# Fewer and larger DMA issues on the SyncE queue in the attention stage of an attention and expert kernel

## The chip, the cores and the metric

The kernel runs on one core of one Trainium2 chip. The metric is the device time of one execution in microseconds (us); the median of several executions is compared.

## The reference, cut to what matters

Eight heads of causal attention over 8 batches of 576 rows, four heads with a local mask (the last 32 positions) and four with a strided one (positions of the same residue modulo 32); the result is the input of a layer of 8 experts, of which each row takes one.

```
scores = scale * q @ k.T                                   # 8 batches, 8 heads, 576 x 576, head size 64
mask_local   = (rel >= 0) & (rel < 32)                      # heads 0 to 3
mask_strided = (rel >= 0) & (pos_k % 32 == pos_q % 32)      # heads 4 to 7
attn = softmax(where(mask, scores, -1e9)); x = (attn @ v) as 4608 rows of 512
e = argmax(x @ w_gate)                                      # one expert a row
out = gate * sigmoid(x @ w_output_gate)[e] * relu(x @ w1[e]) @ w2[e]
```

## The kernel before, in words

The attention stage is a hand-ordered pipeline (the schedule is manual: every engine executes its instructions in the order in which the program writes them). It has 40 steps, t = 0 to 39: batch b = t // 5, and within a batch j = t % 5. A step deals with two windows (w = 0, 1) of up to 128 packed rows. Steps j = 0 and 1 hold strided rows only, j = 3 and 4 local rows only; in j = 2 the first window is strided, and the second holds 64 local and 36 strided rows.

At step t the loop in `attention` (lines 637 to 681) writes, among others: the scores of step t on TensorE (`scores`, L267, into the PSUM tile sp); the normalization of step t-4 on VectorE (`norm`, L329 to L334), which gives the tile x_t; the storing of x_t into the DRAM tensor xd (`rows`, L346 for local rows, L350 for strided rows, on the SyncE queue, called SP); the mask and the maximum of step t on VectorE (`bar` L279, `top` L286); the subtraction on GpSimd (L293), the exponential on ScalarE (L298), the product with the values for step t-3 (`values`, L319), and transposes for later steps. In steps j = 3 and 4 the local values of the batch, one half of the heads each, are copied from vlt to vev, shifted by half a tile (`even`, L229), by VectorE and by ScalarE. Chains for the gate of the experts (`logits`, `gating`) are woven in by `pump`.

The inputs of a batch are read by SP too (`load`, L203): ks and kl (strided and local keys, two halves), qs and ql (strided and local queries, two halves, both into the tile q_t), vs and vl (strided and local values, two halves). All but vl are read for the batch that follows, and there are two buffers of each. `PLAN` says which load is issued in which step and in which part of it: part 2 is at the head of the step (`begin(t, 2)`, L642), parts 0 and 1 stand in `rows` behind the stores of window 0 and window 1. In the steps before t = 4, which have no rows to store, `begin` is called directly. In steps 1 to 4 SP also writes initial entries into the table of rows by expert (`clear`, L97, eight times).

Behind attention come the expert layers: `layer1` (L790), `layer2` (L806) and the scatter of their rows (L823). They read xd by gathers.

Of the kernel before, what the change touches and what calls it, by code (L numbers as in the profile page):

```python
# [17 lines left out]
B, H, S, D = 8, 8, 576, 64  # L18
# [13 lines left out]
NS = 5  # L32
# [20 lines left out]
def attn_moe_kernel(  # L53
# [19 lines left out]
    nc = tc.nc  # L73
# [21 lines left out]
    def clear(e):  # L95

        nc.sync.dma_start(out=table.rearrange("(e p a) w -> e p (a w)", e=E, p=128)[e], in_=empty[0])  # L97
# [68 lines left out]
    def attention():  # L166
        with ExitStack() as actx:
# [20 lines left out]
            def load(b, what, n=None, cs=None):  # L188

                hd = slice(0, 2) if n is None else slice(n, n + 1)  # L190
                cs = cs or slice(0, WS if what == "qs" else S)
                i = b % 2
                if b not in qts:
                    qts[b] = inp.tile([128, 4, WS], F32, name="q_t")
                dst, src = {
                    "ks": lambda: (kbs[i][n::2, :, n, cs], ks[b, n, :, :, cs]),
                    "qs": lambda: (qts[b][:, 2 + hd.start:2 + hd.stop, cs], qs[b, :, hd, cs]),
                    "kl": lambda: (kbl[i][n::2, :, n, :], kl[b, n]),
                    "ql": lambda: (qts[b][:, hd, 0:S], ql[b, :, hd]),
                    "vs": lambda: (vst[i][n::2, n], vs[b, n]),  # L200
                    "vl": lambda: (vlt[i][n::2, n], vl[b, n]),
                }[what]()
                nc.sync.dma_start(out=dst, in_=src)  # L203

            PLAN = {(0, 0): [(1, "ks", 0)], (0, 1): [(1, "ks", 1)], (0, 2): [(0, "vl", 0)],
# [4 lines left out]

            def begin(t, s):
                for d, what, n in PLAN.get((t % NS, s), []):
                    if 0 < t // NS + d < B:
                        load(t // NS + d, what, n)

            zeros = xe[:, 0, 0:256]

# [7 lines left out]
            def even(b, eng, h, f):  # L225

                ps = slice(64 * f, 64 * (f + 1))
                copy = nc.scalar.copy if eng is nc.scalar else eng.tensor_copy
                copy(out=vev[ps, h, f:NL].rearrange("p n i e -> p (n i e)"),  # L229
                     in_=vlt[b % 2][ps, h, 0:NL - f].rearrange("p n i e -> p (n i e)"))  # L230
# [3 lines left out]
            def tiles(j, w):  # L234

                u = 2 * j + w
                local = [(32 * a, 4 * (u - 6) + 2 + a) for a in range(4)] if u > 5 else [(0, 0), (32, 1)] if u == 5 else []
                strided = [(64 * h, 2 * u + 1 + h) for h in range(2)] if u < 5 else [(64, 0)] if u == 5 else []
                return [(p0, 32, n) for p0, n in local] + [(p0, 64, g) for p0, g in strided]
# [98 lines left out]
            def rows(b, j, t=None):  # L338
                x_t = x_[b, j]
                dst = xd[b * S:(b + 1) * S, :]  # L340
                for w in range(2):
                    ts = tiles(j, w)
                    nl = sum(m for _, m, _ in ts if m == 32)
                    if nl:
                        q0 = 32 * ts[0][2]
                        nc.sync.dma_start(out=dst[q0:q0 + nl, 0:256], in_=x_t[0:nl, w, :])  # L346
                    for p0, m, g in ts:
                        if m == 64:
                            r0, nr = resid(g)
                            nc.sync.dma_start(  # L350
                                out=dst[:, 256:512].rearrange("(i r) f -> i r f", r=STRIDE)[:, r0:r0 + nr],
                                in_=x_t[p0:p0 + R * nr, w, :])
                    if t is not None:
                        begin(t, w)

            def resid(g):
                return (0, 2) if g == 0 else (3 * g - 1, 3)
# [225 lines left out]
            def pump():  # L583
                clock[0] += 1
                k = clock[0]
                for c in chains:
                    if k >= c[1]:
                        try:
                            n, z = next(c[0]), 1
                            while n == 0 and (now[0] >= B * NS or z < Z):  # L590
                                n, z = next(c[0]), z + 1
                            c[1] = k + 1 + max(n, 0)
                        except StopIteration:
                            c[1] = 1 << 30
                chains[:] = [c for c in chains if c[1] < 1 << 30]
# [40 lines left out]
            t = 0  # L636
            while t < ns:
                now[0] = t
                live = lambda k: 0 <= t - k < ns
                at = lambda fn, k, *a: fn((t - k) // NS, (t - k) % NS, *a) if live(k) else None  # L640
                b, j = t // NS, t % NS
                begin(t, 2)  # L642
                if 0 < t < 5:
                    clear(2 * t - 2)
                    clear(2 * t - 1)
                at(scores, 0)
                at(norm, 4, 0)
                at(evac_x, 5)
                pump()
                at(norm, 4, 1)  # L650
                pump()
                at(norm, 4, 2)
                if live(4):
                    at(rows, 4, t)
                else:
                    begin(t, 0)
                    begin(t, 1)
                at(bar, 0)
                at(values, 3)
                at(top, 0)  # L660
                at(shift, 0)
                at(turn_p, 2)
                at(turn_x, 4)
                at(evac_p, 2)
                pump()
                pump()
                for h in ((0,) if b and j == 3 else (1,) if b and j == 4 else (0, 1) if t == 4 else ()):
                    even(b, nc.scalar, h, 1)
                    even(b, nc.vector, h, 0)
                at(expo, 0)  # L670
                if t in WIPES:
                    wipe(*WIPES[t])
                if t + 1 < len(WARM):
                    warm(WARM[t + 1])
                pump()
                pump()
                if live(XL) and (t - XL) % NS > 2:
                    chains.append([logits((t - XL) // NS, (t - XL) % NS - 3), 0])
                pump()
                pump()  # L680
                t += 1
# [358 lines left out]
```

## Time and profile before

| | |
|---|---|
| median of 3 runs | 673.96 us (668.85 to 674.24) |
| profiled execution | 675.84 us |
| its span from first to last instruction | 674.1 us |
| mean granted TensorE clock | 0.988 |
| busy share of the span | TensorE 95%, VectorE 46%, ScalarE 40%, GpSimd 29% |

The profile is of one execution. "Busy" leaves out waiting, and DMA issues aren't counted as busy. The 40 slices of the page are 16.85 us each. PE stands for TensorE's matmuls, PEld for its weight loads, DVE for VectorE, ACT for ScalarE, POOL for GpSimd and SPq for SyncE's queue, whose instructions here are issues of DMAs. L12 is line 12 of the kernel.

### The profile page before, as it was taken

The numbers are of one execution on the slowest core, as the hardware profiler recorded it, in microseconds if no ns is written. First come the engines' busy times: TensorE is split into PE (matmuls) and PEld (weight loads), VectorE is DVE, ScalarE is ACT, GpSimd is POOL, SyncE is SP. The second block draws the span as 40 slices with busy tenths as digits, with TensorE's granted clock in tenths as the row PEclk, the third lists the DMA queues.
The fourth block names the chain that finished last, engine by engine and source line by source line (L and its number), as shares of the span: only waits on it lengthen the run. The fifth ranks groups of instructions, "written<-read, shape, count | busy, mean of one in ns | idle before, by whom it ended". The sixth has DMA issues, their size and how long they took to land.

```text
span 674.1 us, 13235 instructions
## 1 busy us (share of the span) xinstructions
PE 639.0 (95%) x5109; PEld 542.4 (80%) x5109; DVE 310.3 (46%) x676; ACT 270.6 (40%) x491; POOL 192.9 (29%) x196
## 2 busy tenths in 40 slices
PE   7889998898898999999999999999999999999995
PEld 5667776777676888988798879889988987987984
DVE  6568887887574224423243224234434423531510
ACT  5755556555543224333333323234234323432410
POOL 5224556556544402201320130024024013111011
PEclk9899999999997999999999999999999999999998
DMA  9977888789342735514251433245245324431001
GB/s 271 347 221 212 259 249 238 243 247 315 95 131 78 226 103 150 162 32 141 85 155 44 132 110 124 77 124 166 64 122 171 98 87 119 144 108 41 2 13 41
DMA packets 47849, 96.86 MB, mean 144 GB/s; under 512 B 9076, under 2 KB 19844, under 8 KB 47786
## 3 DMA queue, kind: packets, MB, share of 16 engines
q1 hardware_dynamic: 38330, 72.58, 36.2%
q0 software_dynamic: 8048, 20.05, 8.9%
q10 hardware_dynamic: 1408, 3.38, 1.5%
q8 instruction: 41, 0.67, 0.4%
q14 instruction: 22, 0.18, 0.1%
HBM read 74.44 MB, written 22.38 MB: 144 GB/s over the span
## 4 chain that ended last, share of the span: by engine, by line
PE 56%; issue 21%; DVE 6%; DMA 6%; POOL 5%; ACT 3%; SPq 1%; POOLq 0%; DVEq 0%; ACTq 0%
PE yp L806 23%; PE hp L790 21%; PE xp L319 4%; DMA q_t<-in_qs_dram 3%; PE sp L267 2%; POOL out_dram L823 2%; PE tp L780 2%; PE tp L305 1%; DVE p_t L279 1%; DVE st L286 1%; POOL xg L151 1%; PE xtp L364 1%; DMA vlt<-in_vl_dram 1%; PE gp L396 1%; POOL p_t L293 1%
## 5 line engine op out<-in xcount | busy, mean ns | idle before, releaser
L790 PE MATMUL hp<-xh,w1l 128*128 128x256 f32 (+1 forms) x480 | 147.9, 308 | 0.0
L790 PE MATMUL hp<-xl,w1h 128*128 128x256 f32 (+1 forms) x480 | 147.8, 308 | 0.0
L790 PE MATMUL hp<-xh,w1h 128*128 128x256 f32 (+1 forms) x480 | 147.8, 308 | 0.0
L823 POOL DMA_INDIRECT out_dram<-ys,tab x40 | 41.9, 1046 | 353.4 <-ACT ys L822 342.1
L790 PEld LDWEIGHTS hp<-xh,w1h 128*128 128x128 f32 x480 | 91.0, 190 | 2.1
L790 PEld LDWEIGHTS hp<-xl,w1h 128*128 128x128 f32 x480 | 91.0, 190 | 1.9
L790 PEld LDWEIGHTS hp<-xh,w1l 128*128 128x128 f32 x480 | 90.9, 189 | 1.4
L806 PE MATMUL yp<-w2h,hhb 128*128 128x512 f32 (+3 forms) x208 | 83.9, 403 | 0.0
L806 PE MATMUL yp<-w2l,hhb 128*128 128x512 f32 (+3 forms) x208 | 82.0, 394 | 0.0
L806 PE MATMUL yp<-w2h,hlb 128*128 128x512 f32 (+3 forms) x208 | 81.6, 393 | 0.0
L728 DVE TENSOR_TENSOR xl<-tp,xh 128x512 fp32r<-128x512 f32 (+3 forms) x40 | 25.7, 650 | 120.0 <-ACT xh L727 119.8
L727 ACT CAST xh<-tp 128x512 fp32r<-128x512 f32 (+3 forms) x40 | 21.9, 555 | 130.4 <-PE tp L780 130.4
L794 DVE SCALAR_TENSOR_TENSOR hlb<-hp,hhb 128x480 fp32r<-128x480 f32 (+7 forms) x64 | 34.6, 541 | 84.6 <-ACT hhb L793 84.6
L793 ACT ACTIVATE hhb<-hp 128x480 fp32r<-128x480 f32 (+7 forms) x64 | 30.6, 478 | 102.8 <-PE hp L790 102.8
L293 POOL TENSOR_TENSOR p_t<-p_t,st 128x512 f32<-128x512 f32 x40 | 47.4, 1186 | 75.2 <-DVE st L286 20.1
L806 PE MATMUL yp<-w2h,hha 128*128 128x512 f32 x128 | 52.1, 407 | 0.0
L806 PE MATMUL yp<-w2h,hla 128*128 128x512 f32 x128 | 51.3, 400 | 0.0
L151 POOL DMA_INDIRECT xg<-xd,tab x40 | 46.7, 1168 | 15.6 <-issue 10.1
L806 PE MATMUL yp<-w2l,hha 128*128 128x512 f32 x128 | 51.1, 399 | 0.0
L563 POOL DMA_INDIRECT table<-meta,dst x48 | 44.7, 931 | 20.8 <-issue 10.2
L794 DVE SCALAR_TENSOR_TENSOR hla<-hp,hha 128x256 fp32r<-128x256 f32 x56 | 23.6, 421 | 54.8 <-ACT hha L793 54.8
L822 ACT ACTIVATE ys<-yp,tab 128x512 f32<-128x512 f32 (+3 forms) x40 | 27.7, 693 | 48.2 <-issue 28.5
(147 smaller groups left out, 1076.9 us busy)
## 6 DMA issues: line engine op xcount, KB each, us to landing
raw<-in_moe_w_dram SPq DMA_DIRECT2D x54, 512.0 KB
vst<-in_vs_dram SPq DMA_DIRECT2D x16, 357.5 KB
vlt<-in_vl_dram SPq DMA_DIRECT2D x16, 292.5 KB
xd<-x_t SPq DMA_DIRECT2D x80, 54.0 KB
q_t<-in_qs_dram SPq DMA_DIRECT2D x14, 293.0 KB
xd<-x_t SPq DMA_DIRECT2D x32, 128.0 KB
q_t<-in_ql_dram SPq DMA_DIRECT2D x14, 288.0 KB
raw<-in_moe_w_dram ACTq DMA_DIRECT2D x6, 512.0 KB
```

What stands on the lines that cost most here:

```text
L151: nc.gpsimd.indirect_dma_start(out=dst, out_offset=None, in_=src, in_offset=bass.IndirectOffsetOnAxis(ap=idx, axis=0), bounds_check=top, o ...
L293: nc.gpsimd.tensor_tensor(out=p_t, in0=p_t, in1=st.unsqueeze(2).to_broadcast([128, 4, 64, 2]), op=ALU.subtract)
L319: nc.tensor.matmul(out=xp[p0:p0 + m, w, 130 * i:130 * (i + 1)], lhsT=pt[:, w, i, p0:p0 + m], rhs=value(b, i, m, n), start=True, stop=True)
L563: i = nc.gpsimd.indirect_dma_start(out=table[:, :], out_offset=bass.IndirectOffsetOnAxis(ap=dst[:, j:j + 1], axis=0), in_=meta[:, b * NB + ...
L727: nc.scalar.copy(out=hi, in_=src)
L728: nc.vector.tensor_tensor(out=lo, in0=src, in1=f32(hi), op=ALU.subtract)
L790: nc.tensor.matmul(out=hp[:, 0:n], lhsT=w[:, k, 128 * j:128 * (j + 1)], rhs=x[:, k, 0:n], start=first, stop=(k == KC - 1 and w is w1l))
L793: nc.scalar.activation(out=hh[:, j, 0:n], in_=hp[:, 0:n], func=AF.Relu)
L794: nc.vector.scalar_tensor_tensor(out=hl[:, j, 0:n], in0=hp[:, 0:n], scalar=0.0, in1=f32(hh[:, j, 0:n]), op0=ALU.max, op1=ALU.subtract)
L806: nc.tensor.matmul(out=yp[0:m, :], lhsT=h[:, j, o:o + m], rhs=w[:, j, :], start=(j == 0 and q == 0), stop=(j == FC - 1 and q == 2))
L822: nc.scalar.activation(out=ys[0:m, :], in_=yp[0:m, :], func=AF.Copy, scale=f32(tab[:, 1:2]))
L823: i = nc.gpsimd.indirect_dma_start(out=out[:, :], out_offset=bass.IndirectOffsetOnAxis(ap=tab[:, 0:1], axis=0), in_=ys[0:m, :], in_offset= ...
```

## The change: larger loads and stores, and a new order

Three things are done. The local rows of the steps j = 3 and j = 4, two windows of 128 rows, are stored by one DMA instead of two. The two halves of the strided queries of a batch are one load, and so are the two halves of the local queries. The loads of a batch, now ten, are dealt out anew, one to each of the two parts 0 and 1 of the five steps; part 2, at the head of a step, is gone. The local rows of a step are now stored ahead of its strided rows.

```
-            PLAN = {(0, 0): [(1, "ks", 0)], (0, 1): [(1, "ks", 1)], (0, 2): [(0, "vl", 0)],
-                    (1, 0): [(1, "qs", 0)], (1, 1): [(1, "qs", 1)], (1, 2): [(0, "vl", 1)],
-                    (2, 0): [(1, "kl", 0)], (2, 1): [(1, "kl", 1)],
-                    (3, 0): [(1, "ql", 0)], (3, 1): [(1, "ql", 1)],
-                    (4, 0): [(1, "vs", 0)], (4, 1): [(1, "vs", 1)]}
+            PLAN = {(0, 0): (1, "ks", 0), (0, 1): (0, "vl", 0), (1, 0): (1, "ks", 1), (1, 1): (0, "vl", 1),
+                    (2, 0): (1, "qs", None), (2, 1): (1, "kl", 0), (3, 0): (1, "kl", 1), (3, 1): (1, "ql", None),
+                    (4, 0): (1, "vs", 0), (4, 1): (1, "vs", 1)}
 
             def begin(t, s):
-                for d, what, n in PLAN.get((t % NS, s), []):
-                    if 0 < t // NS + d < B:
-                        load(t // NS + d, what, n)
+                d, what, n = PLAN[t % NS, s]
+                if 0 < t // NS + d < B:
+                    load(t // NS + d, what, n)
...
             def rows(b, j, t=None):
                 x_t = x_[b, j]
                 dst = xd[b * S:(b + 1) * S, :]
+                if j > 2:
+                    q0 = 256 * j - 704
+                    nc.sync.dma_start(out=dst[q0:q0 + 256, 0:256].rearrange("(w p) f -> p w f", w=2), in_=x_t)
+                elif j == 2:
+                    nc.sync.dma_start(out=dst[0:64, 0:256], in_=x_t[0:64, 1, :])
                 for w in range(2):
-                    ts = tiles(j, w)
-                    nl = sum(m for _, m, _ in ts if m == 32)
-                    if nl:
-                        q0 = 32 * ts[0][2]
-                        nc.sync.dma_start(out=dst[q0:q0 + nl, 0:256], in_=x_t[0:nl, w, :])
-                    for p0, m, g in ts:
+                    for p0, m, g in tiles(j, w):
                         if m == 64:
                             r0, nr = resid(g)
                             nc.sync.dma_start(
...
                 b, j = t // NS, t % NS
-                begin(t, 2)
                 if 0 < t < 5:
                     clear(2 * t - 2)
```

## Rows read from the trace of the kernel before

**Rows 1.** The page: busy time, share of the span and instructions of each engine; then the granted TensorE clock and the busy share of the DMA engines in 40 equal slices, in tenths.

```profile
PE 639.0 (95%) x5109; PEld 542.4 (80%) x5109; DVE 310.3 (46%) x676; ACT 270.6 (40%) x491; POOL 192.9 (29%) x196
...
PEclk9899999999997999999999999999999999999998
DMA  9977888789342735514251433245245324431001
```

**Rows 2.** The chain of work that ended last, in order of time: start, duration (us), what. A DMA's piece goes from its issue to its landing.

```profile
18.79 4.95 DMA q_t<-in_qs_dram
...
41.31 4.57 DMA q_t<-in_qs_dram
...
103.05 5.35 DMA q_t<-in_qs_dram
...
218.72 20.93 PE hp L790 x96
```

**Rows 3.** The timeline of TensorE, the scores of the steps 5, 10 and 20 to 25: start, duration (us), engine, line, operation, tiles, shapes, count; in brackets the idle time before it and what ended it.

```profile
23.13 0.44 PE L267 MATMUL sp<-kbs,q_t 128*64 128x128 f32 x4 [2.58 <-DMA q_t<-in_qs_dram]
23.77 1.55 PE L267 MATMUL sp<-kbs,q_t 128*64 128x128 f32 x12 [0.20 <-DMA q_t<-in_qs_dram]
...
43.09 0.44 PE L267 MATMUL sp<-hha,q_t 128*64 128x128 f32 x4
45.92 0.88 PE L267 MATMUL sp<-hha,q_t 128*64 128x128 f32 x12 [2.39 <-DMA q_t<-in_qs_dram]
...
86.59 1.09 PE L267 MATMUL sp<-hha,q_t 128*64 128x128 f32 x16
...
90.58 1.10 PE L267 MATMUL sp<-hha,q_t 128*64 128x128 f32 x16
...
94.75 1.09 PE L267 MATMUL sp<-hha,q_t 128*64 128x128 f32 x12
...
98.82 1.08 PE L267 MATMUL sp<-hla,q_t 128*32 128x128 f32 x32
...
103.09 1.06 PE L267 MATMUL sp<-hla,q_t 128*32 128x128 f32 x32
...
107.09 0.44 PE L267 MATMUL sp<-kbs,q_t 128*64 128x128 f32 x4
108.44 0.88 PE L267 MATMUL sp<-kbs,q_t 128*64 128x128 f32 x12 [0.91 <-DMA q_t<-in_qs_dram]
```

**Rows 4.** SP's issues by line, over the whole span: the line, the transfer and the number of issues; the time that an issue took (least, median, most, in ns); the start of the first and the last (us). L203 is loads, L350 strided rows, L346 local rows.

```profile
L203 SPq DMA_DIRECT2D q_t<-in_qs_dram x16: 397/458/1663, 0.9 to 144.3; - x16
L203 SPq DMA_DIRECT2D vst<-in_vs_dram x16: 532/534/808, 6.9 to 156.5; - x16
L203 SPq DMA_DIRECT2D vlt<-in_vl_dram x16: 524/538/1392, 8.2 to 163.1; - x16
L203 SPq DMA_DIRECT2D q_t<-in_ql_dram x15: 424/464/1097, 4.9 to 151.2; - x15
...
L203 SPq DMA_DIRECT2D kbs<-in_ks_dram x8: 552/589/593, 13.5 to 139.5; - x8
...
L350 SPq DMA_DIRECT2D xd<-x_t x88: 725/758/1645, 26.1 to 180.6; - x88
...
L346 SPq DMA_DIRECT2D xd<-x_t x40: 319/492/2452, 39.9 to 183.8; - x40
```

**Rows 5.** The timeline of SP: start, duration (us) of an issue, line, transfer, count. The first is the load of all local queries of batch 0 in one issue.

```profile
4.90 0.61 SPq L203 DMA_DIRECT2D q_t<-in_ql_dram  x1
...
26.07 1.72 SPq L350 DMA_DIRECT2D xd<-x_t  x2
...
82.79 0.46 SPq L203 DMA_DIRECT2D q_t<-in_qs_dram  x1
...
98.13 1.33 SPq L203 DMA_DIRECT2D vlt<-in_vl_dram  x1
99.56 1.59 SPq L350 DMA_DIRECT2D xd<-x_t  x2
...
104.67 2.45 SPq L346 DMA_DIRECT2D xd<-x_t  x1
```

**Rows 6.** Windows of the attention stage: the stretch, its length, the busy time of each engine (instructions), the granted clock, the share of the DMA engines and what they moved (GB/s).

```profile
24.00:28.00 4.00, 4.00 (x36) 3.46 (x35) 1.62 (x4) 1.29 (x3) 0.97 (x1) 0.61 1.04 403
...
87.00:108.00 21.00, 18.90 (x303) 14.78 (x298) 17.65 (x49) 12.46 (x28) 12.15 (x13) 1.00 0.84 248
```

**Rows 7.** DMA issues by size: the table's clears and the stores of local rows.

```profile
xd<-x_t SPq DMA_DIRECT2D x32, 128.0 KB
...
table<-raw SPq DMA_DIRECT2D x8, 296.0 KB
```

**Rows 8.** The timeline of VectorE: the copies of the local values in the steps 8 and 9, the x_t of step 21, and the second copy of the local values of batch 4, in step 24.

```profile
38.05 0.75 DVE L229 COPY vev<-vlt 64x1170 f32<-64x1170 f32 x1
...
41.62 0.75 DVE L229 COPY vev<-vlt 64x1170 f32<-64x1170 f32 x1
...
91.86 0.69 DVE L334 TENSOR_TENSOR x_t<-xp,rs 128x512 f32<-128x512 f32 x1
...
105.63 0.75 DVE L229 COPY vev<-vlt 64x1170 f32<-64x1170 f32 x1
```

## Prediction

> **What bounds the kernel now.** I read the page first. TensorE is busy for 95% of the span, and its granted clock is full in nearly every slice [rows 1]. The DMA digits are 7 to 9 in the first ten slices and, but for one, 0 to 5 behind them [rows 1], so there are two stages: attention, up to about 190 us, and the expert layers behind it. The chain in order of time confirms the second: from 218.72 us on it runs through matmuls of the experts [rows 2]. Nothing of the change is left there, so I count it unchanged.
>
> In attention the chain is carried by matmuls and VectorE, but at a few places it passes through a strided query load that had not landed: issued at 18.79, at 41.31 and at 103.05 us, landing 4.95, 4.57 and 5.35 us later [rows 2]. The timeline of TensorE shows the price of each: the scores of steps 5, 10 and 25, each the first step of a batch, stood for 2.58 + 0.20, 2.39 and 0.91 us [rows 3]. These 6.1 us are all that late loads cost TensorE.
>
> Between them the loop keeps a beat of its own: 86.59, 90.58, 94.75, 98.82, 103.09, 107.09 us are the starts of six successive scores [rows 3], that is 3.99 + 4.17 + 4.07 + 4.27 + 4.00 = 20.50 us a batch without a stall. In such a batch TensorE works 18.9 and VectorE 17.65 of 21 us [rows 6]; no load is in that beat.
>
> Why do those loads come late? SP's timeline: the second query half is issued at 82.79 and again at 103.05 us [rows 2, 5], 20.26 us for 28 issues. By the medians [rows 4] these are 2 x (0.458 + 0.534 + 0.538 + 0.464) + 4 x 0.589 (keys) = 6.34 us of loads, 11 strided stores x 0.758 = 8.34, 5 local stores x 0.492 = 2.46: 17.14 us. The other 3.1 us, 0.11 an issue, are gaps and issues that took long without a cause that I can read, as the 2.45 us and the 1.33 us [rows 5]. So SP issues for 20.26 of 20.50 us and never catches up: the x_t written at 91.86 + 0.69 = 92.55 us [rows 8] gets its first store issued at 99.56 [rows 5], 7.0 us later. The queue is late, not the engines short of transfers: their share is 0.84 there [rows 6].
>
> **The change part by part.** *Fewer issues.* Per batch 28 become 24: two local stores, one query half of each kind. In the whole kernel 8 x 2 + 7 x 2 = 30. What the merged ones cost is not in the trace; the whole local query load of the start is one issue of 0.61 us [rows 5] against 2 x 0.464, and I take 0.61 for both merged queries. The merged store has a third dimension: at least a local store (0.492), at most two of them (0.98); I take 0.70, near the strided one at 0.758, which also has an extra dimension. Then SP has 5.72 + 8.34 + 0.49 + 2 x 0.70 = 15.95 us and 24 x 0.11 = 2.64: 18.6 us a batch. It gains 20.5 - 18.6 = 1.9 us a batch on the loop; if the merged ones cost as much as their two halves, only 0.45 + 0.24 = 0.7. By itself this is worth nothing: SP is waited for through late loads alone.
>
> *Start, step 5.* The strided queries of batch 1 move from step 1 to step 2, behind two more table clears of 296 KB [rows 7]. The DMA engines are full there (share 1.04, 403 GB/s [rows 6]), so two clears are 2 x 303 / 403 = 1.5 us. The second half landed at 23.7 us; the whole one lands at 25.2. Also, all 16 matmuls of the scores now wait for it; before, four ran at 23.13, the rest from 23.77 to 25.32 [rows 3]. All 16 take 1.09 us [rows 3], so they end at 25.3 + 1.1 = 26.4: **+1.0 us** at step 5, with bounds 0 and +2.9 (the clears' bandwidth halved by what else is queued).
>
> The wait for both halves is where a page speaks against the change. The trace shows matmuls of the first query half running at 23.13 and 43.09 us while the second had not landed [rows 3]. The Trainium skill, "DMA: Bandwidth & Descriptors", section "Why a DMA increments its semaphore by 16 and not by 1", says that only the full count tells that a transfer has landed, so nothing of a merged load can be used early. By that rule the four matmuls lose their head start, 0.4 us at a step that waits; the sum above has it.
>
> *Step 10.* SP's 20 issues from 26.07 us [rows 5] up to this load are 20 in both kernels. In the new order they are 11 strided stores (8.34), two loads each of vs, vl and ks (3.32), one local and one merged store (1.19), with gaps of 0.06 to 0.11 14.1 to 15.1 us; in the start two issues fewer stand ahead, up to 0.5 us earlier. The whole query load is issued at 39.7 to 41.2. It lands after 4.57 to 5.35 us, as the halves did [rows 2], plus the second half's 300 KB at 403 down to 248 GB/s [rows 6], 0.7 to 1.2 us: between 45.0 and 47.8. I take 45.8, near the middle, since the low ends belong to a queue without long issues. Before, the second half released 12 matmuls at 45.92 which took 0.88; now 16 follow 45.8 with 1.09: **+0.1 us**, bounds -0.7 and +2.1. The +1.0 of step 5 disappears in this wait: the loop would ask at 43.09 + 1.0 = 44.1, before the landing.
>
> *Local values, steps 8 and 9.* Their loads move from the head of a step to its end, behind four stores and a key load: 4 x 0.758 + 0.589 = 3.6 us, and gaps. They are issued at about 34.2 and 38.4 us and land (4.57 to 5.35) at 38.8 to 39.6 and 43.0 to 43.7. The copies to vev asked at 38.05 and 41.62 [rows 8], now 1.0 later: 39.05 and 42.6. So the second may hold up VectorE, and ScalarE's copy behind it, by 0.4 to 1.1 us; queued behind them are the normalization, the mask of step 10 and the exponential. Step 10's scores wait for queries until 45.8 anyway: **0**, and up to 1.1 if that cover is gone.
>
> *Step 25.* Three batches later SP has gained 3 x 1.9 = 5.7 us (bounds 2.1 and more), the whole load needs up to 1.2 more. The 0.91 us of stall go in full: **-0.9 us**. With the lower bounds it is 2.1 - 1.2 = 0.9, just enough. What is late next is nothing: the beat of 20.50 us goes on.
>
> *Moved loads with no effect.* Second half of the strided keys a step later, local keys a half step, local queries at the end of step 3: each has two steps (8 us) or more to its use, against some 5 us of landing. Local rows ahead of strided rows: both wait for the same x_t, and its buffer is asked for five steps later, 20.5 us.
>
> Sum: +0.1 - 0.9 = -0.8 us on a span of 674.1 (the profiled execution took 675.84, so 675.0). That execution was 1.9 us above the median; I put the sum on the median: 673.96 - 0.8 = **673.1 us**.
>
> **The rivals.** *SP stays late, values come late (slower).* If SP gains nothing, for instance because long issues scale with the size of a transfer, the local values are the trap. The second half was issued at 98.13 and used at 105.63 [rows 5, 8]: 7.5 us, of which landing takes 4.57 to 5.35, so 2.2 to 2.9 are left. Issued 3.6 us later it is 0.7 to 1.4 us late, in each of the batches 1 to 7, in front of VectorE's and ScalarE's queues: 7 x 1.05 = 7.4, with step 25's stall kept: about 681 us. It decides where SP gains less than about 1 us in all by then. Against it: 30 issues less, and a beat that needs 20.50 where SP would need 18.6.
>
> *All waits go (faster).* If a merged load lands as fast as a half and the start's clears don't delay it, the 2.58 + 0.20 + 2.39 + 0.91 go: 668 us, no more, since the beat stays. Against it: the DMA engines are full when step 5's load is queued [rows 6]. The Trainium skill's page just named, section "Rules for kernel authors", advises to coalesce small transfers since overhead dominates them; by it this case would be the likely one. The trace does not bear it out: issues follow each other every 0.5 to 0.8 us while each takes 4.6 us or more to land [rows 2, 4], so their fixed parts overlap.
>
> *No effect.* The stall of step 10 only shifts, that of step 25 stays: 674 us.
>
> **How the numbers follow.** Chances: forecast 0.72, no effect 0.13, all waits go 0.08, SP stays late 0.07. A change of this kernel under about 1% can't be told from none (the runs shown lie 0.8% apart); forecast, no effect and nearly all of the faster case are inside it, and half of the slower case: within 1% 0.92, faster 0.03, slower 0.05. The range: the forecast's bounds are -0.7 - 0.9 = -1.6 and +2.1 + 1.1 = +3.2; the low runs of before, 5 us under the median, and the faster case pull the lower end to 669.0; the upper end is 677.2.
>
> **What would show it.** Right: scores of step 5 start some 2 us later than 23.13, step 10's end near 47 as before, no stall on a query load after it; the lag between x_t and its first store shrinks from 7 us to about the wait for x_t itself by 110 us; 24 issues per batch, 18 to 19 us of SP. Wrong: waits of VectorE or ScalarE on the local values beyond step 9, a beat other than 20.5 us, a merged store that takes over 1 us to issue, or a second stretch at the lower of the two clock levels after the longer stop of TensorE at step 5 (24 to 28 us has a granted clock of 0.61 now [rows 6]; as much again would cost 4 x 0.39 = 1.6 us).

## The result and the profile after

The changed kernel takes 676.14 us (median of 20 executions, 673.06 to 680.05), the kernel before 673.34 us beside it (20 executions): ratio 1.0059, 95% interval 1.0041 to 1.0076. It is 2.8 us slower where 0.8 us of gain were forecast; the time lies inside the range, the sign is wrong.

The profiled execution took 675.56 us with a span of 673.9 us, no more than the one of before (675.84 and 674.1). The two traces can't be subtracted from end to end: the profiled execution of before lay 2.5 us above its median, and each execution has its own stretches of lower clock, as shown below. So I compare stage by stage. One execution of the runs below (of ids_before), at 1044.44 us with a granted clock of 0.557, is a slow one and left out of its ratio. The page of the changed kernel, TensorE's busy time, then the granted clock in 40 slices [rows 1]:

```profile
PE 637.9 (95%) x5109; PEld 541.6 (80%) x5109; DVE 310.9 (46%) x676; ACT 270.5 (40%) x491; POOL 192.4 (29%) x196
...
PEclk9799999999998999999999999999999999999998
```

The timeline of TensorE in the changed kernel, the scores (L265) of the steps 5, 10, 11, 25 and 35 to 37 and one matmul in between; in brackets the idle time before and what ended it [rows 3]:

```profile
25.50 1.98 PE L265 MATMUL sp<-kbs,q_t 128*64 128x128 f32 x16 [5.08 <-DMA q_t<-in_qs_dram]
...
45.47 1.09 PE L265 MATMUL sp<-hha,q_t 128*64 128x128 f32 x16
...
49.46 1.10 PE L265 MATMUL sp<-hha,q_t 128*64 128x128 f32 x16
...
107.03 1.09 PE L265 MATMUL sp<-kbs,q_t 128*64 128x128 f32 x16
...
148.64 1.09 PE L265 MATMUL sp<-kbs,q_t 128*64 128x128 f32 x16
...
153.64 1.09 PE L265 MATMUL sp<-kbs,q_t 128*64 128x128 f32 x16
...
157.25 0.27 PE L317 MATMUL xp<-vev,pt 128*32 128x130 f32 x1 [2.52 <-DVE x_t L332]
...
159.31 0.88 PE L265 MATMUL sp<-kbs,q_t 128*64 128x128 f32 x10
```

The same places in the kernel before, from step 35 on:

```profile
149.69 1.09 PE L267 MATMUL sp<-kbs,q_t 128*64 128x128 f32 x16
153.68 1.10 PE L267 MATMUL sp<-kbs,q_t 128*64 128x128 f32 x16
156.17 0.27 PE L319 MATMUL xp<-vev,pt 128*32 128x130 f32 x1 [1.40 <-DVE x_t L334]
158.23 1.09 PE L267 MATMUL sp<-kbs,q_t 128*64 128x128 f32 x12
```

At step 35 the changed kernel is 149.69 - 148.64 = 1.05 us ahead, near the 0.8 us forecast. Two steps later it is 1.08 us behind: 8.54 us became 10.67. No load ends a wait there. The place to look at is GpSimd, whose subtraction every step needs. GpSimd in the kernel before, then in the changed one, from step 32 on: the read of the small table `tabe` for the step ahead (DMA_DIRECT2D), the subtractions of steps 33, 34 and 36 (TENSOR_TENSOR), and scatters into `table`:

```profile
142.38 0.59 POOL L453 DMA_DIRECT2D tabe<-table  x1 [0.56 <-issue]
144.51 1.46 POOL L293 TENSOR_TENSOR p_t<-p_t,st 128x512 f32<-128x512 f32 x1 [1.53 <-DVE dst L556]
146.49 0.95 POOL L563 DMA_INDIRECT table<-meta,dst  x1 [0.52 <-DVE x_t L334]
147.75 1.33 POOL L563 DMA_INDIRECT table<-meta,dst  x1 [0.31 <-issue]
149.10 1.05 POOL L293 TENSOR_TENSOR p_t<-p_t,st 128x512 f32<-128x512 f32 x1
...
158.58 1.06 POOL L293 TENSOR_TENSOR p_t<-p_t,st 128x512 f32<-128x512 f32 x1
```

```profile
141.92 0.59 POOL L451 DMA_DIRECT2D tabe<-table  x1 [1.14 <-issue]
143.46 1.46 POOL L291 TENSOR_TENSOR p_t<-p_t,st 128x512 f32<-128x512 f32 x1 [0.95 <-DVE dst L554]
147.98 0.95 POOL L561 DMA_INDIRECT table<-meta,dst  x1 [3.06 <-DVE st L284]
149.24 0.92 POOL L561 DMA_INDIRECT table<-meta,dst  x1 [0.30 <-DMA q_t<-in_ql_dram]
150.19 1.05 POOL L291 TENSOR_TENSOR p_t<-p_t,st 128x512 f32<-128x512 f32 x1
...
159.66 1.06 POOL L291 TENSOR_TENSOR p_t<-p_t,st 128x512 f32<-128x512 f32 x1
```

The read is issued 0.46 us earlier than before, yet GpSimd stands 3.06 us ahead of the scatter that follows, where it was 0.52. The releasers printed there are others. The scatter writes the table that the read reads, and waits for it; the profile has no row of the landing, so I read it from the trace's semaphore events. The last of the read's 16 increments comes at 145.66 us before and 147.15 after, 3.28 and 5.23 us behind the issue, and GpSimd's wait on that semaphore, a separate instruction ahead of the scatter, ends 0.03 us later in both; it lasted 1.15 us before and 3.68 after. From that scatter on GpSimd has no slack: subtraction 34 to subtraction 36 takes 9.48 and 9.47 us, filled with four scatters and two gathers, so whatever the read loses arrives at step 37.

The second place is the start. Windows of 22 to 32 us, before and after (columns as in [rows 6]; the clock stands behind the five engines):

```profile
22.00:32.00 10.00, 8.59 (x101) 6.89 (x101) 5.23 (x12) 6.84 (x11) 1.62 (x2) 0.83 1.01 371
```

```profile
22.00:32.00 10.00, 6.50 (x60) 5.56 (x60) 3.07 (x6) 4.37 (x8) 1.04 (x1) 0.66 0.98 348
```

TensorE stood for 5.08 us ahead of step 5, and the lower of the two clock levels (1.2 of 2.4 GHz) was granted from 22.94 to 29.77 us instead of 23.71 to 27.12: 6.83 us against 3.41.

### The profile page after: what moved, and what is told of

It reads as the page before. It is cut to its first block, busy times and chain, and to the rows that moved or that the text cites. A ratio compares the mean times of both kernels' runs of the same rounds, so it can differ in the third digit from the quotient of the medians.

```text
span 673.9 us, 13205 instructions
## 1 busy us (share of the span) xinstructions
PE 637.9 (95%) x5109; PEld 541.6 (80%) x5109; DVE 310.9 (46%) x676; ACT 270.5 (40%) x491; POOL 192.4 (29%) x196
## 4 chain that ended last, share of the span: by engine, by line
PE 45%; issue 20%; POOL 3%; DMA 1%; POOLq 0%
PE yp L803 23%; PE hp L787 21%; POOL out_dram L820 2%; PE tp L777 2%; POOL xg L151 1%; DMA xg<-xd,tab 1%; POOL table L561 0%; POOLq L820 0%; POOLq L905 0%; POOLq L151 0%
```

## The experiments

All ratios are to the kernel before on the same chip. In the list, t5, t11 and t35 are the starts of the scores of these steps, "35-37" the time from scores 35 to scores 37, "read" the landing of tabe's read behind its issue, "low" the time at the lower clock ahead of the experts' first full layer (us, one trace each). The three runs on a chip where the kernel before took 701.71 us don't stand in it:

```
kernel          ratio  [95%]             t5     t11    t35     35-37  read  low
before          1                        23.13  49.54  149.69   8.54  3.28  10.2
before_again                             22.70  50.30  149.47   8.54  3.48   6.8
before_third                             23.87  50.00  149.14   8.46  3.18   6.8
rows_only       1.0004 [0.9988, 1.0020]  23.71  49.04  148.23   8.53  3.39   3.4
queries_only    0.9997 [0.9972, 1.0021]  23.62  47.23  146.41  11.26  4.53   6.8
old_order       0.9998 [0.9977, 1.0018]  23.47  48.49  147.66  10.72  4.85   6.8
after           1.0059 [1.0041, 1.0076]  25.50  49.46  148.64  10.67  5.23  10.2
after_again     1.0058 [1.0036, 1.0079]  24.86  48.93  148.06  10.48  4.66  10.2
early_queries   1.0062 [1.0036, 1.0088]  23.00  50.93  150.07  11.88  4.67  10.2
late_weights    1.0044 [1.0021, 1.0068]  25.35  49.52  148.68  11.28  4.44  13.7
halves          1.0071 [1.0046, 1.0097]  25.14  50.44  149.56  10.57  5.13   6.8
swap_last       1.0050 [1.0030, 1.0070]  25.41  49.91  149.03  12.00  5.00  13.7
swap            1.0053 [1.0031, 1.0075]  24.11  48.72  147.82  11.08  4.35  13.7
tabe_early      1.0025 [1.0011, 1.0040]  25.49  52.91  152.07  10.40  2.85   6.8
ids_after       1.0007 [0.9990, 1.0023]  26.24  51.02  150.14   8.27    -    3.4
ids_before      0.9986 [0.9968, 1.0004]  22.64  47.78  146.92   8.26    -    3.4
free_old_again  0.9973 [0.9953, 0.9994]  22.49  46.25  145.41   8.25  4.71   0.0
```

**The change again, and its parts at the start.** The changed kernel as it is:

> The changed kernel once more, for a second trace and a measured ratio beside the experiments. Theory A (the start pays): step 5 starts again near 25.5 us instead of 23.1, behind two more table clears, with a stretch at the lower clock level of some 6.8 us instead of 3.4; ratio to the kernel before about 1.004 to 1.006. Theory B (the end of attention pays): the GpSimd read of the table (tabe) lands 5 us after its issue instead of 3.3, the subtraction of step 34 starts more than 5 us after its scores instead of 3.4, and steps 36 and 37 come 2 us later relative to step 34. In the one trace of the changed kernel both are seen; a second one tells whether they are there each time.

The table clears of steps 1 to 4 behind the step's loads:

```
-                if 0 < t < 5:
-                    clear(2 * t - 2)
-                    clear(2 * t - 1)
...
                     begin(t, 1)
+                if 0 < t < 5:
+                    clear(2 * t - 2)
+                    clear(2 * t - 1)
```

> The changed kernel, but in steps 1 to 4 SP writes the table clears behind the loads of the step instead of ahead of them, so the whole strided query load of batch 1 has two clears ahead of it, as its second half had before. Theory A: step 5 starts at 23.5 to 24.0 us instead of 25.5, the stretch at the lower clock is 3.4 us, and the time falls by 2 to 3 us against the changed kernel (ratio to before 1.000 to 1.002). Theory B: step 5 is earlier by as much, but the time falls by less than 1 us unless the lead survives the GpSimd waits at steps 34 to 37.

The four loads of the first weights, in the step ahead, each issued a step later:

```
-                for c in range(4):
-                    if c > 1:
+                for c in range(5):
+                    if c in (2, 3):
...
-                    load_w(0, 1, cs=[c])
+                    if c:
+                        load_w(0, 1, cs=[c - 1])
```

> The changed kernel, but the four loads of the first expert's weights (L160, 512 KB each), which start beside the GpSimd read of the table, are issued one step later. Theory B: the read of the table lands 3 to 4 us after its issue, the subtraction of step 34 starts some 3.5 to 4 us after its scores, steps 36 and 37 follow as in the kernel before (4.0 and 4.55 us), and the time falls by 1 to 2 us against the changed kernel. Theory A: no change beyond 0.5 us.

The queries in two halves again, in the new places:

```
-                    (2, 0): (1, "qs", None), (2, 1): (1, "kl", 0), (3, 0): (1, "kl", 1), (3, 1): (1, "ql", None),
+                    (2, 0): (1, "qs", (0, 1)), (2, 1): (1, "kl", 0), (3, 0): (1, "kl", 1), (3, 1): (1, "ql", (0, 1)),
...
-                    load(t // NS + d, what, n)
+                    for k in n if isinstance(n, tuple) else (n,):
+                        load(t // NS + d, what, k)
```

> The changed kernel with both query loads split into their two halves again, at the same two places of the order (12 loads in 10 places, the merged store of local rows stays). If merging a load costs (theory C: nothing of a merged load can be used before all of it has landed), the first four matmuls of step 5 start near 24.7 us instead of 25.5, and the time falls by up to 0.5 us. If only the order and the clears count (theory A), step 5 ends its scores at the same 27.5 us and the time is that of the changed kernel within 0.5 us.

The loss repeats (676.31 us, 1.0058). Step 5 back at 23.00 us does not mend it, though it doesn't clear the start either: step 10 of early_queries then waits 1.45 us for its queries, and step 11 starts 1.5 us later than in the changed kernel. Whole or half queries make no difference, and later weights gain 0.0014, inside the intervals. Each of the four has its 10.5 to 11.9 us between the scores 35 and 37.

**The kernel before, twice more**, for its own spread:

> The kernel before once more, for a second trace of it. The trace on record is of an execution 2.5 us above the median of the runs, so something in it is not typical. If step 10's stop of 2.4 us or step 25's of 0.9 us is missing here, the forecast took from the change a gain that the usual execution of before never had to give (theory D). If both are there, the difference lies behind attention: the stretch at the lower clock at the start of the experts, 6.8 us in that trace.

> The kernel before a third time, for the same question: which of the stops at steps 5, 10 and 25, of the waits at steps 34 to 37 and of the stretches at the lower clock are there in each execution.

They took 674.53 and 673.93 us. Steps 35 to 37 are the same in all three traces (8.46 to 8.54), the start is not (t11 from 49.54 to 50.30), and step 25's stall of 0.91 us [rows 3] is in the first trace alone. In before_again the scores of step 25 run in one piece:

```profile
107.84 1.09 PE L267 MATMUL sp<-kbs,q_t 128*64 128x128 f32 x16
```

**The read earlier, and the merged store alone.** GpSimd's read half a step earlier in the changed kernel, and the kernel before with nothing but the merged store:

```
             def ahead():
-                yield 4
+                yield 0
```

> The changed kernel, but GpSimd reads the table (tabe) half a step earlier in its order, ahead of the large loads and of the subtraction of step 32, where SP's traffic is light. Theory B (SP, now on time, puts 1.1 MB of loads and stores just ahead of this small read, so that it lands 4.4 to 5.2 us after its issue instead of 3.3, and GpSimd's next scatter stands in front of the subtraction of step 34): the subtraction of step 34 starts some 3 to 3.5 us after its scores instead of 5.4, steps 35 to 37 take 8.5 to 9 us instead of 10.5 to 10.7, and the time falls by 1.5 to 2.5 us against the changed kernel, ratio to before 1.000 to 1.003. Theory A or any other: less than 0.5 us.

```
+                if j > 2:
+                    q0 = 256 * j - 704
+                    nc.sync.dma_start(out=dst[q0:q0 + 256, 0:256].rearrange("(w p) f -> p w f", w=2), in_=x_t)
...
-                    if nl:
+                    if nl and j == 2:
```

> The kernel before with the merged store of local rows alone, all loads in their old places. If the loss comes from SP being on time (theory B), this one, which saves 2 issues of 28 per batch, some 0.8 us, catches up slowly; its lag at step 32 should lie between 7 and 2 us and its time between before and after, ratio 1.000 to 1.004. If the new order of loads makes the loss (theory A at the start), the ratio is 0.997 to 1.000.

The earlier read lands in 2.85 us and over half of the loss is gone (1.0025). The scatter no longer waits for it (0.04 us). Its one trace, of the slowest of its 12 executions, still takes 10.40 us from step 35 to 37, with a gather now ahead of subtraction 34, so it doesn't show where the gain lies. The merged store alone changes nothing (1.0004).

**Which neighbour delays the read.** The strided queries and the second half of the strided keys exchanged, for the last batch only or for all, and the merged queries alone in the kernel before:

```
+                if t // NS == B - 2 and s == 0 and t % NS in (1, 2):
+                    d, what, n = PLAN[3 - t % NS, s]
```

> The changed kernel, but for the last batch that is loaded the whole strided query load is dealt to step 31 and the second half of the strided keys to step 32, the other way round. Theory A (the strided queries, issued 3 us ahead of GpSimd's read of tabe, are what makes that read land 5.2 us after its issue): the read lands in 3.3 to 3.8 us, the subtraction of step 34 starts 3.4 to 4.0 us behind its scores instead of 5.5, the steps 35 to 37 take 8.5 to 9.3 instead of 10.7 us, ratio 1.001 to 1.004. Theory B (any queue that is on time does it, since weights, local keys, local queries and the merged store remain around the read): the read stays over 4.3 us, 35 to 37 at 10 us or more, ratio 1.005 to 1.007. Theory C (the loss lies in the first ten steps): no difference, 1.005 to 1.007, whatever the read does.

```
-            PLAN = {(0, 0): (1, "ks", 0), (0, 1): (0, "vl", 0), (1, 0): (1, "ks", 1), (1, 1): (0, "vl", 1),
-                    (2, 0): (1, "qs", None), (2, 1): (1, "kl", 0), (3, 0): (1, "kl", 1), (3, 1): (1, "ql", None),
+            PLAN = {(0, 0): (1, "ks", 0), (0, 1): (0, "vl", 0), (1, 0): (1, "qs", None), (1, 1): (0, "vl", 1),
+                    (2, 0): (1, "ks", 1), (2, 1): (1, "kl", 0), (3, 0): (1, "kl", 1), (3, 1): (1, "ql", None),
```

> The changed kernel with the strided queries in step 1 and the second half of the strided keys in step 2 of every batch, the other way round. Theory A: as the run before at steps 34 to 37; the start gains besides, scores of step 5 at 23 to 24.5 instead of 25.5; ratio 0.999 to 1.003. Theory B: over 1.004. Theory C: the start gains 1 us or more against the run before, so the ratio falls by 0.0015 or more between the two.

```
-                    (1, 0): [(1, "qs", 0)], (1, 1): [(1, "qs", 1)], (1, 2): [(0, "vl", 1)],
+                    (1, 0): [(1, "qs", None)], (1, 2): [(0, "vl", 1)],
...
-                    (3, 0): [(1, "ql", 0)], (3, 1): [(1, "ql", 1)],
+                    (3, 0): [(1, "ql", None)],
```

> The kernel before with the two halves of the strided queries as one load at the place of the first half, the local ones likewise; nothing else. Theories A and B: merging as such costs nothing, ratio 0.998 to 1.003; SP is 1 us a batch ahead of before or less. If whole loads themselves cost (all matmuls wait for the whole): scores of steps 5 and 10 start 1 us or more later than 23.1 to 23.9 and 42.1 to 43.9, ratio 1.003 to 1.006.

Of the theories of these three runs, A falls: without the strided queries the read still takes 5.00 us. Theory B, an on-time queue, falls in part: in queries_only SP is 4.6 to 6.4 us late at steps 31 to 35, and the read takes 4.53 us all the same, its last increment 1.4 us behind the one before; and rows_only, only 0.7 to 3.2 us late at the same steps, has its read in 3.39 us. Theory C, a loss in the first ten steps, isn't borne out: swap starts step 11 1.2 us earlier than swap_last, and its ratio is no lower. Yet queries_only isn't slower: it is 3.3 us ahead of before at step 35, and what the end takes it had gained at the start.

**The forms without the order, and the wait taken away.** Both merged forms in the old order (the two edits rows_only and queries_only together); then, in the kernel before and the changed one, the read at its old place from the input of row numbers, which no scatter writes:

> The kernel before with both merged forms, the local rows of two windows in one store and the strided and the local queries in one load each, everything at its old place in the old order. If the new order is the cause: ratio 0.997 to 1.002 although SP has 30 issues fewer; SP's lag shrinks by about 2 us a batch as in the changed kernel. If the merged forms together (a queue that is on time, whatever its order) are the cause: ratio 1.004 to 1.007, the read of tabe lands over 4.3 us after its issue and the steps 35 to 37 take over 10 us.

```
-                nc.gpsimd.dma_start(out=tabe, in_=src.rearrange("o (p c) w -> p (o c) w", p=128))
+                nc.gpsimd.dma_start(out=tabi[0:QB], in_=ids_in[:, 0:EH // 128, :])
...
-                        fetch(xgs[c - 2], xd[0:EB * S, :], tabe[:, c - 2, 0:1], EB * S - 1)
+                        fetch(xgs[c - 2], xd[0:EB * S, :], tabi[:, c - 2, 0:1], EB * S - 1)
...
                 fillers.append(lead_layer())
+                nc.gpsimd.dma_start(out=tabe, in_=src.rearrange("o (p c) w -> p (o c) w", p=128))
```

> The changed kernel without the wait under dispute: at the old place GpSimd reads the same amount not from the table of rows but from the input that holds the row numbers, which no scatter writes, so the next scatter into the table waits for no read; the gathers of the step ahead take these row numbers, 96 of 128 (a part of the computation is changed: the first rows of one expert). The true read of the table follows behind attention's end. If the read of tabe holds up GpSimd: the subtraction of step 34 starts 3 us or less behind its scores (5.5 in the changed kernel), the steps 35 to 37 take 8 to 9 us, ratio 1.000 to 1.003. If the loss lies elsewhere: ratio 1.005 or more.

> The kernel before with the same edit (row numbers from the input in place of the table for the step ahead, the true read of the table behind attention's end). It waited 1.1 us for that read. If the read of tabe is the whole loss of the changed kernel: ratio 0.997 to 1.000 here, and the one with the change is no more than 0.001 above it. If the start of attention or its clock carries part of the loss: the difference of the two remains at 0.002 to 0.004. If the read is not the cause: the difference remains at 0.005 or more.

Without the wait, steps 35 to 37 take 8.27 and 8.26 us, and the difference of the two kernels falls from 0.0059 to 1.0007 - 0.9986 = 0.0021, which the intervals don't tell from nothing but which lies at the low end of what was expected if the start carries a part of the loss. The merged forms in the old order cost nothing (0.9998), although their read is as late (4.85 us).

**The wait alone taken away, nothing else.** The read takes the first 256 rows of an expert that has them by then; the scatters behind it write others. So it is declared independent of them:

```
+                reads.append(nc.gpsimd.dma_start(out=tabe, in_=src.rearrange("o (p c) w -> p (o c) w", p=128)))
...
                     distinct(i, scatters)
+                    for read in reads:
+                        tc.declare_no_dep(i.ins, read.ins, reason="the read takes rows that are written by then")
```

> The changed kernel with GpSimd's read of tabe declared independent of the scatters that come after it: they write rows of the table that the read doesn't take (the expert that is read has its 256 rows by then). Nothing is left out. If the scatter's wait for the read is the cause: 1.7 us or less from the scores of step 34 to its subtraction, steps 35 to 37 in 8.2 to 8.6 us, ratio 0.999 to 1.002 as with the row numbers from the input. If the busy queue around the read delays GpSimd in another way too (its gathers and scatters): steps 35 to 37 over 9 us, ratio over 1.003.

> The kernel before with the same edit. It waited 1.1 us, and has little to gain: ratio 0.997 to 1.000. The difference of the run above to this one is what the change costs without that wait: 0 to 0.002 if the wait is the cause, 0.004 or more if not.

> Both merged forms in the old order, with the same edit. The old order kept the start's gain (scores of step 11 at 48.5 instead of 49.5 to 50.3 us) and lost it again in the steps 35 to 37 (10.7 us instead of 8.5). Without the wait those 2 us stay: ratio 0.995 to 0.998, the best of all kernels. If the order has no part in the loss: the same as the changed kernel with the edit, 0.999 to 1.002.

These three fell on a chip on which the kernel before itself took 701.71 us: 0.9982 [0.9950, 1.0015], 1.0007 [0.9981, 1.0034] and 0.9987 [0.9954, 1.0019], all three the same as before. On that chip the steps are longer from step 15 on, and with no wait for the read the steps 35 to 37 still take 12.04, 17.60 and 14.03 us, so something else ends them there. The three decide nothing for the others, and the changed kernel with this edit has no run on a usual chip. The last run repeats the third on a usual one:

> The kernel of the run before this once more, on another chip, since on that one the kernel before itself took 701.71 us, with longer steps from step 15 on. Both merged forms in the old order, the scatters no longer waiting for the read of tabe. If that wait and the new order are the two halves of the loss: steps 35 to 37 in 8.2 to 8.6 us, ratio 0.995 to 0.998. If the forms at their old places with the wait (0.9998) have nothing to gain from it: 0.999 to 1.001.

669.98 us against 672.69, ratio 0.9973 [0.9953, 0.9994]: as expected, and faster than the kernel before. Against old_order (0.9998, on another chip) the intervals overlap. GpSimd there, the same lines as above:

```profile
138.40 0.59 POOL L457 DMA_DIRECT2D tabe<-table  x1 [0.85 <-issue]
140.22 1.47 POOL L294 TENSOR_TENSOR p_t<-p_t,st 128x512 f32<-128x512 f32 x1 [1.23 <-DVE dst L560]
141.84 0.95 POOL L567 DMA_INDIRECT table<-meta,dst  x1 [0.15 <-DVE x_t L335]
143.10 0.92 POOL L567 DMA_INDIRECT table<-meta,dst  x1 [0.30 <-issue]
144.18 1.40 POOL L294 TENSOR_TENSOR p_t<-p_t,st 128x512 f32<-128x512 f32 x1 [0.16 <-PE tp L306]
...
154.01 1.06 POOL L294 TENSOR_TENSOR p_t<-p_t,st 128x512 f32<-128x512 f32 x1
```

The read still lands 4.71 us behind its issue, at 143.11 us. The scatter doesn't wait for it any more (0.15 us idle instead of 3.06), and TensorE's stop behind it is 1.11 us instead of 2.52:

```profile
149.39 1.09 PE L268 MATMUL sp<-kbs,q_t 128*64 128x128 f32 x16
151.60 0.27 PE L320 MATMUL xp<-vev,pt 128*32 128x130 f32 x1 [1.11 <-DVE x_t L335]
153.66 1.10 PE L268 MATMUL sp<-kbs,q_t 128*64 128x128 f32 x12
```

**What the clock took.** Every execution has its mean granted clock; (1 - clock) x span is an estimate of the time that TensorE loses to the lower level, the end of the kernel included. For the 20 executions of the changed kernel it is 6.78 us at a mean span of 674.7; for 112 executions of the kernel before, on five chips, 4.82 us at 671.1. So some 2.0 of the 3.6 us between them are clock. Without the wait (ids_after) it is 5.15 us, beside 5.10 of the kernel before on that chip. But the wait alone doesn't bring it: in the old order old_order has 4.98 and queries_only 5.15 us, with 10.72 and 11.26 us in steps 35 to 37. The other kernels of the new order have 5.74 to 8.09 us. In single traces, a stretch of the lower clock that starts between 153.9 and 160.4 us stands in seven of the ten of the list in which steps 35 to 37 take over 10 us, and in none of the seven in which they take 8.54 or less. Windows of 150 to 162 us in old_order and in free_old_again:

```profile
150.00:162.00 12.00, 9.50 (x134) 7.68 (x128) 7.79 (x23) 5.06 (x16) 7.50 (x8) 0.86 0.84 287
```

```profile
150.00:162.00 12.00, 10.69 (x181) 8.69 (x177) 10.91 (x38) 5.96 (x16) 6.38 (x7) 1.00 0.74 247
```

## Why the prediction was wrong, point by point

- **SP's gain: right, larger than said.** SP's issues in the changed kernel by line (columns as in [rows 4]), first the stores (L348 strided rows, L341 the merged store, L343 the 64 local rows of j = 2), then the query loads:

```profile
L348 SPq DMA_DIRECT2D xd<-x_t x88: 725/744/1412, 25.5 to 181.6; - x88
L341 SPq DMA_DIRECT2D xd<-x_t x16: 365/504/1292, 39.6 to 184.5; - x16
L343 SPq DMA_DIRECT2D xd<-x_t x8: 493/500/547, 35.3 to 179.5; - x8
```

```profile
L203 SPq DMA_DIRECT2D q_t<-in_qs_dram x9: 391/407/698, 0.9 to 139.0; - x9
L203 SPq DMA_DIRECT2D q_t<-in_ql_dram x8: 554/604/1130, 4.9 to 143.2; - x8
```

  A merged store takes 0.50 us (0.70 assumed), a merged query load 0.41 and 0.60 (0.61). The lag of 7.0 us is gone: the x_t of step 21 is written at 91.78 + 0.69 = 92.47, its store issued at 92.50:

```profile
91.78 0.69 DVE L332 TENSOR_TENSOR x_t<-xp,rs 128x512 f32<-128x512 f32 x1
```

```profile
92.50 0.49 SPq L343 DMA_DIRECT2D xd<-x_t  x1
```

- **Step 5: direction right, size too small.** 25.50 us where 25.2 was said for the landing, but the 16 matmuls took 1.98 us instead of 1.09, at the lower clock, and the next step came 2.4 us later than before. The sum had +1.0 (bounds to +2.9). By the Trainium skill ("DMA: Bandwidth & Descriptors", "Why a DMA increments its semaphore by 16 and not by 1") only the full count tells that a transfer has landed, so nothing of a merged load can be used early. The trace agrees: x16 in one piece behind the wait. It has no weight in the time: halves, with a load and a semaphore for each half, is at 1.0071.
- **Step 10: the number right, by luck.** Its last scores end at 45.47 + 1.09 = 46.56 (46.9 forecast), and step 11 starts within 0.1 us of before, but no load decides it. The whole query load was issued at 40.24, as said, and by its semaphore events its last increment came at 44.85, under the 45.0 to 47.8 said. TensorE got to these scores at 45.47 and waited for nothing. The loss of 2.4 us at step 5 had eaten the 2.39 us that step 10 waited before; two errors, in the loss at step 5 and in the landing, cancelled.

```profile
40.24 0.40 SPq L203 DMA_DIRECT2D q_t<-in_qs_dram  x1
```

- **Step 25: the stall is gone, but the gain was none.** Scores 26 start at 111.02 instead of 112.06 us. But two of the three traces of before have no stall at step 25, so the -0.9 us, the sum's only gain, was read from one execution that the two others don't bear out.

```profile
111.02 1.09 PE L265 MATMUL sp<-kbs,q_t 128*64 128x128 f32 x16
```

```profile
112.06 1.10 PE L267 MATMUL sp<-kbs,q_t 128*64 128x128 f32 x16
```

- **The second stretch of low clock at the start** was named among what would make it wrong, at 1.6 us. It came in five of nine traces of the new order and in none of eight of the old one; what it cost lies where before step 10 waited, and is a part of the 2.4 us above.
- **"What is late next is nothing: the beat of 20.50 us goes on": this step failed.** The beat does go on, 86.51 to 107.03 us (scores 20 to 25) is 20.52 us. But I took it for attention up to its end, and never looked at steps 32 to 37, where GpSimd has the step ahead besides. There a read that lands 2 us later became the wait that ends last: steps 35 to 37 took 10.67 instead of 8.54 us, a term of +2.1 us that the sum put at nothing without a reason. I followed what SP's stores and loads release, and judged the moved loads by their own deadlines alone.
- **The rivals.** The slower one (values late) didn't come. The faster one needs the start undelayed and the wait gone: free_old_again is that, 2.7 us below the kernel before, of 6 said. The Trainium skill's rule to coalesce ("DMA: Bandwidth & Descriptors", "Rules for kernel authors") is for small transfers: under 64 KB one pays mostly overhead. The halves merged here were 128 KB (stores) and 288 to 293 KB (loads), so it didn't make this case the likely one, against what the prediction drew from it; and 14 merged query loads and 16 merged stores by themselves gave nothing, 0.9998.

The account of the loss, then. The three traces of before start step 35 at 149.4 us in the mean. In the old order the merged forms start it 1.2 to 4.0 us earlier, but with one trace each, and the old forms did so by 2.5 in one (ids_before). Where the queries are merged and the wait stands, they lose 2 us or more between the scores 35 and 37: 0.9997 and 0.9998. The changed kernel starts step 35 only 0.8 and 1.4 us earlier, and the wait and the lower clock take more than that: 1.0059.

That the wait makes the steps 35 to 37 long is shown by taking it away: 8.27 us in ids_after, 8.25 in free_old_again. That it makes the time is shown by ids_after, 1.0007 in place of 1.0059 (its gathers take other rows, too); 0.9973 in place of 0.9998 points the same way within the intervals. That the new order has a part is shown by old_order, 0.9998 with the same merged forms and a wait. Its place isn't shown: most traces of the new order lose time at step 5, but early_queries, where step 5 waits 0.58 us, stays at 1.0062.

Three things stay open. First, which piece of the order it is: the strided queries back in step 1 leave 1.0053, but in that trace (swap) step 5 waits 4.24 us for the strided keys instead. Second, which transfers delay the read: neither these queries (swap_last) nor the weights (late_weights) do it alone. At its old place it lands in 3.18 to 3.48 us in the four traces with the two halves of the queries apart, and in 4.35 us or more wherever they go out together, as one load or one behind the other; that is no proof. Third, why the kernels of the new order have more lower clock, ids_after alone excepted.

## What to carry to other kernels

When an edit moves the transfers of a queue in time, look at the stretch with the least slack on any engine, not at the mean beat, and list there the small reads that an engine waits for in order. Before a dependence between a read and later writes is paid for, see whether they touch the same rows at all; here taking that wait away changed the ratio by 0.0052 (ids_after), while the 30 issues fewer by themselves changed nothing (0.9998). And read several executions before two traces are subtracted: the one trace of before had 3.4 us more of lower clock than its two repeats.

## What the hardware showed

A read of 256 short rows (16 KB) by GpSimd landed 2.85 to 5.23 us behind its issue in 15 traces of the same read; in all 13 traces where a scatter into the same table waited for it, that wait ended 0.03 us behind the last of its 16 increments. One increment can be late alone (4.53 us where the other 15 had come in 3.15, queries_only). In the traces of the list the lower clock came in stretches of 3.41 or 6.83 us ahead of the kernel's end, among others around TensorE's stops of 5.08 us at step 5 (the changed kernel) and 2.32 us at step 36 (tabe_early); the changed kernel's stop of 2.52 us at step 36 had none. So the same kernel differs by one or two stretches, at half the clock 1.7 us for each 3.41, from one execution to the next. One of the chips ran the same kernel in 701.71 us: between 80 and 140 us the instructions lasted as long as elsewhere (VectorE's mask 620 ns in free_before, 603 in the trace of before) and the waits between engines were longer, and by the sum above the lower clock took 12.9 us there.
